# A hand-ordered one-core kernel: the same 633 tasks in another order, 63 of them on another engine

## The chip, the cores and the metric

The kernel runs on one core of one Trainium2 chip. The metric is device time in microseconds (us), median of the runs; lower is better. Five instruction queues matter: PE (TensorE, matmuls; its weight loads are listed as PEld), ACT (ScalarE), DVE (VectorE), POOL (GpSimd) and SP (SyncE, which here only issues DMAs).

## The reference

What is computed, cut to its core: a layer norm of x (2048 rows of 448), a linear recurrence over the rows (a state-space scan) on one branch, a two-layer MLP with a second layer norm on the other, and a gated sum.

```python
def _A_ref(x, ...):                                  # recurrence, L = 2048
    Lam_bar = jnp.exp(dt * Lam)
    B_bar = ((Lam_bar - 1.0) / Lam)[:, None] * Bmat
    Bu = jnp.einsum("bld,pd->blp", x + 0j, B_bar)
    for t in range(L):
        h = Lam_bar[None, :] * h + Bu[:, t, :]
    y = 2.0 * jnp.einsum("blp,dp->bld", hseq, Cmat).real + x * Dskip
def _B_ref(x, w1, b1, w2, b2):                       # MLP, F = 1792
    y = _layernorm(x)
    h = _gelu(jnp.einsum("bsd,df->bsf", y, w1) + b1)
    return jnp.einsum("bsf,fd->bsd", h, w2) + b2
xn = _layernorm(x)
return x + _A_ref(xn, ...) * silu(_B_ref(xn, ...))
```

## The kernel before

The 2048 rows are worked in four groups (g = 0 to 3) of 512 rows: two blocks of 128 partitions with two rows (even and odd, "par") each. The scan runs over pairs of rows, so even and odd rows get different output matrices.

The program is a list of 633 tasks. A task is one or a few instructions of one engine, with the names of what it reads and writes. `link` derives from these names, in the order of creation, which task depends on which. `emit` then issues the tasks in the order of a hand-kept list, `ORDER`; each engine's queue is the subsequence of `ORDER` that belongs to it, and an engine takes its instructions strictly in that order. Tasks added by `either` have two forms for two engines (DVE or ACT, POOL or DVE); the numbers in the list `SECOND` take the second form. Nothing else sets the order: there are no priorities at run time.

Waits are placed by `emit`. A task waits for the semaphore of every task it depends on, except for one shortcut (line 129): a PE task does not wait for an earlier PE task, unless one of them is marked `split`.

```python
for d in sorted(t.deps, key=at.get, reverse=True):
    if t.eng == d.eng == "pe" and not (t.split or d.split):
        continue
    sem, val = done[d]
    if seen.get(sem, 0) < val:
        waits.append((sem, val))
```

The PE tasks that are marked `split` are those of the first MLP product, `mm1_run` (matmul line 801). One pass of it over a group has seven steps j = 0 to 6, and a step fills two PSUM banks (the bank pairs are 0/1, 2/3 and 4/7, used in turn). A step is cut in two phases. The first, called **Fj** below, has six matmuls of 64 weight rows that start the two accumulations; the second, **Sj**, has eight that finish them. The two row halves of the array change banks between Fj and Sj, and both write the same two banks, so Sj depends on Fj and waits for its semaphore. After Sj come two gelus on ACT (line 805), which write `gT`; the next step on the same bank pair depends on them. For group 0 the pass is cut in three: steps 0 to 4 for the first 128-row block (256 columns a matmul; marked a), steps 5 and 6 for both blocks, steps 0 to 4 for the second block (marked b). All other passes have 512 columns. The phases are tasks 113 to 153, 286 to 305, 409 to 428 and 537 to 556.

Other PE tasks: `mm2` (line 828, second MLP product, 14 matmuls, two PSUM banks in turn, drained by DVE line 831), `bu` (line 729, input product of the scan, four tasks a group, all in bank 4, drained into `u_sb` at line 417), `m0` (line 712, a product of CQ and B, once), `ym` (lines 871, 874 and 877, the output product, bank 7 nearly throughout, drained by DVE lines 883, 885 and 888). The scan between `bu` and `ym` is on DVE (lines 744 to 775, with `s_w` scanned at 753). CQ and CZ (line 661) are output matrices with the discretisation worked in, made by DVE and ACT from `Ct0` to `Ct3`, which are DMA transposes issued by SP (line 83), as are `BT` (transposed input matrices), `xnT` and `xmT` (transposed normalised rows; `xmT` is the tile xn2T). SP's plain DMAs (line 84) load x, the weights and B, C, and store the output. `dbc` (a skip vector) is loaded by POOL and halved by task 45 on DVE.

Of the kernel before, what the change touches and what calls it, by code (L numbers as in the profile page):

```python
# [159 lines left out]


ORDER = [int(k) for k in """
# [17 lines left out]
""".split()]  # L180
SECOND = [int(k) for k in """
45 53 54 61 63 66 69 74 76 83 112 130 133 158 160 162 163 165 177 184 185 187 189 190 220 222 224 226 228 230 238 248 249 258 266 268 331 362 364 365
384 400 401 436 447 468 480 482 487 491 499 501 502 504 510 528 529 609 612 627
""".split()]


# [834 lines left out]
```

## Time and profile before

| what | value |
|---|---|
| time, median of 3 runs | 153.23 us (153.21 to 153.32) |
| span of the profiled execution | 151.8 us, 2974 instructions |
| PE busy | 147.1 us (97%), 1127 matmuls |
| DVE busy | 127.6 us (84%) |
| ACT busy | 99.0 us (65%) |
| POOL busy | 42.1 us (28%) |
| granted TensorE clock | full throughout |

The profile is of one execution, whose span from the first to the last instruction is 151.8 us. The 1.4 us to the median lie outside the span; the profile gives no other time of that execution. Times in the views count from the start of the span.

### The profile page before, as it was taken

To read this page: it belongs to the slowest core of one execution; us is meant where nothing else is said; L and a number is where in the kernel's file an instruction comes from. 1 tells how busy PE (TensorE), PEld (TensorE's weight loads), DVE (VectorE), ACT (ScalarE), POOL (GpSimd) and SP (SyncE) were. 2 spreads that over 40 slices of the span, in tenths; PEclk is the share of its full clock that TensorE was granted. 3 is DMA by queue.
4 is the path that set the end of the run, shared out by engine and by line. 5 is a ranking of instruction groups with operands and counts; after the bars stand their busy time and mean duration, and the time that the engine had idled before them with its cause. 6 is when DMAs were issued, how large, how long until landed. Compare 5 with 4: busy or idle time off the path is not lost.

```text
span 151.8 us, 2974 instructions
## 1 busy us (share of the span) xinstructions
PE 147.1 (97%) x1127; PEld 86.6 (57%) x1127; DVE 127.6 (84%) x267; ACT 99.0 (65%) x183; POOL 42.1 (28%) x101
## 2 busy tenths in 40 slices
PE   7899999999999999999999999999999999999992
PEld 7785755454566577545444556764454666555551
DVE  2874999999978979999999996379968726999984
ACT  3888996988789559997898610463579834067400
POOL 5376827153020920010456006200072031000201
PEclk9999999999999999999999999999999999999999
DMA  4999999989997300700003032610331001100022
GB/s 116 262 305 390 266 202 138 219 152 133 165 261 180 65 0 0 138 0 4 0 0 63 4 60 45 154 60 4 60 101 23 0 4 57 64 0 0 4 84 98
DMA packets 31236, 14.73 MB, mean 97 GB/s; under 512 B 24752, under 2 KB 30774, under 8 KB 31222
## 3 DMA queue, kind: packets, MB, share of 16 engines
q1 hardware_dynamic: 30912, 14.26, 41.8%
q0 software_dynamic: 160, 0.23, 1.0%
q8 instruction: 9, 0.15, 0.4%
q10 hardware_dynamic: 150, 0.05, 0.1%
q14 instruction: 5, 0.04, 0.1%
HBM read 6.89 MB, written 1.84 MB: 57 GB/s over the span
## 4 chain that ended last, share of the span: by engine, by line
PE 80%; DVE 9%; DMA 4%; SPq 4%; issue 2%
PE psum L828 23%; PE psum L801 22%; PE psum L729 14%; PE psum L871 13%; DMA x_all<-in_A_x_dram 4%; PE psum L874 4%; SPq L84 4%; PE psum L712 3%; DVE xn_sb L499 2%; DVE lnst L399 1%; DVE s_w L628 1%; PE psum L877 1%; DVE o L831 1%; PE psum L697 1%; DVE tmp L891 1%
## 5 line engine op out<-in xcount | busy, mean ns | idle before, releaser
L801 PE MATMUL psum<-xn2T,w_sb 64*128 64x512 bf16 (+1 forms) x462 | 44.6, 345 | 0.3 <-ACT xn2T L417 0.2
L828 PE MATMUL psum<-w_sb,gT 128*128 128x448 bf16 x224 | 44.5, 353 | 0.2 <-DVE o L831 0.2
L805 ACT ACTIVATE gT<-psum,b1f 128x512 bf16<-128x512 f32 (+1 forms) x66 | 35.9, 625 | 10.4 <-PE psum L801 10.2
L801 PEld LDWEIGHTS psum<-xn2T,w_sb 64*128 64x128 bf16 x462 | 24.1, 109 | 19.8 <-ACT gT L805 2.3
L828 PEld LDWEIGHTS psum<-w_sb,gT 128*128 128x128 bf16 x224 | 21.5, 98 | 20.7 <-DVE o L831 0.6
L417 ACT ACTIVATE u_sb<-psum 128x512 bf16<-128x512 f32 (+2 forms) x22 | 10.5, 478 | 23.0 <-PE psum L729 22.7
L729 PE MATMUL psum<-xnT,BT 128*128 128x256 bf16 x196 | 24.0, 273 | 0.0
L729 PEld LDWEIGHTS psum<-xnT,BT 128*128 128x128 bf16 x196 | 18.9, 98 | 5.4 <-issue 1.1
L891 POOL TENSOR_TENSOR tmp<-t,x_all 128x448 bf16<-128x448 bf16 x5 | 5.2, 1032 | 33.1 <-DVE t L888 30.7
L753 DVE TENSOR_TENSOR_SCAN s_w<-dk,vs 128x774 f32<-128x774 f32 x8 | 14.0, 1760 | 0.1
L500 ACT ACTIVATE xn_sb<-x_all,lnw 128x448 bf16<-128x448 bf16 (+2 forms) x21 | 13.0, 662 | 1.2 <-DVE xn_sb L499 1.1
L417 ACT ACTIVATE vs<-s_w 64x256 bf16<-64x256 f32 (+2 forms) x16 | 10.9, 681 | 2.6 <-DVE s_w L753 1.5
L871 PE MATMUL psum<-CZ,h_sb 128*128 128x448 bf16 x56 | 11.9, 352 | 0.0
L871 PE MATMUL psum<-CQ,h_sb 128*128 128x448 bf16 (+2 forms) x54 | 10.5, 332 | 0.0
L399 DVE BATCH_NORM_STATS2 lnst<-x_all 128x6 f32<-128x448 bf16 x12 | 7.1, 617 | 3.4 <-DMA x_all<-in_A_x_dram 3.4
L831 DVE TENSOR_TENSOR o<-psum,b2bc 128x448 f32<-128x448 f32 x16 | 9.7, 614 | 0.2
L871 PEld LDWEIGHTS psum<-CZ,h_sb 128*128 128x128 bf16 x56 | 5.4, 98 | 4.7 <-DVE lnmv L405 0.4
L871 PEld LDWEIGHTS psum<-CQ,h_sb 128*128 128x128 bf16 x54 | 5.1, 98 | 4.0 <-DVE t L885 0.4
L874 PE MATMUL psum<-M,xnT 128*128 128x448 bf16 x32 | 7.4, 352 | 0.0
L480 POOL TENSOR_TENSOR lnw<-lnw,mhalf 128x8 f32<-128x8 f32 x3 | 7.2, 2404 | 0.3
L883 DVE TENSOR_TENSOR Cr<-psum,xd 128x448 f32<-128x448 f32 x7 | 4.3, 620 | 3.5 <-PE psum L877 3.4
L499 DVE TENSOR_SCALAR xn_sb<-x_all,lnw 128x448 bf16<-128x448 bf16 (+2 forms) x19 | 6.9, 396 | 0.0
(160 smaller groups left out, 189.1 us busy)
## 6 DMA issues: line engine op xcount, KB each, us to landing
out_dram<-tmp SPq DMA_DIRECT2D x7, 224.0 KB, 2.0
x_all<-in_A_x_dram SPq DMA_DIRECT2D x3, 448.0 KB, 4.0
w_sb<-in_B_w_dram SPq DMA_DIRECT2D x3, 448.0 KB, 8.4
w_sb<-in_B_w_dram SPq DMA_DIRECT2D x3, 384.0 KB, 4.8
vs<-in_A_C_re_dram SPq DMA_DIRECT2D x1, 392.0 KB, 11.6
Bn<-in_A_B_im_dram SPq DMA_DIRECT2D x1, 336.0 KB, 10.2
Bn<-in_A_B_re_dram SPq DMA_DIRECT2D x1, 336.0 KB, 10.5
vs<-in_A_C_im_dram SPq DMA_DIRECT2D x1, 336.0 KB, 10.8
```

The source lines that it names most:

```text
L399: dve([lambda e, b=b, par=par, q=q: e.bn_stats(lnst[:, q, :], x_all[:, 2 * g + b, par, :])], [f"x{2 * g + b}"] , [f"st{q}"], 0.62, prio)
L417: kb.either(("act", [lambda e, o=o, i=i: e.activation(o, i, ACT.Copy) for o, i in pairs]), ("dve", [lambda e, o=o, i=i: e.tensor_copy(o, i ...
L499: on = [("dve", [lambda e, o=o, i=i: e.tensor_scalar(o, i, rs, nb, op0=ALU.mult, op1=ALU.add) for o, i in parts], 0.4, 0.12), ("act", [lam ...
L500: ("act", [lambda e, o=o, i=i: e.activation(o, i, ACT.Identity, bias=nb, scale=rs) for o, i in parts], 0.75, 0.2)]
L729: fns = [lambda e, r=r, m=m, d=d: e.matmul(psum[:, 4, r * NK:(r + 1) * NK], BT[:, m, d, :], xnT[:, gx, d, :], start=(d == 0), stop=(d == 6 ...
L753: dve(lambda e, so=so, vi=vi: e.tensor_tensor_scan(so, dk[:].rearrange("p i c -> p (i c)"), vi, 0.0, ALU.mult, ALU.add), ["v", "vl", "dk", ...
L801: return lambda e: e.matmul(view(bk[k]), w1_sb[rows, d, fcol(2 * j + k)], rhs[rows, d, :, :], start=not second and n == 0, stop=second and ...
L805: act([lambda e, k=k: e.activation(gT[:, gb, 2 * j + k, :].rearrange("p (r c) -> p r c", r=2)[:, :, cols], view(bk[k]), ACT.Gelu_apprx_tan ...
L828: fns = [lambda e, fi=fi: e.matmul(psum[:, bk, 0:D], gT[:, gb, fi, q * 128:(q + 1) * 128], w2_sb[:, fi, :], start=(fi == 0), stop=(fi == N ...
L831: dve(lambda e: e.tensor_tensor(o2[:, fb, :], psum[:, bk, 0:D], b2bc[:], ALU.add), [f"ps{bk}", "b2bc"], [f"oo{fb}"], 0.62, prio - 76)
L871: fns = [lambda e, k=k: e.matmul(psum[:, bk, c0:c1], h_sb[:, hb, k, k0:k0 + 128], cm[:, k, c0:c1], start=(k == 0), stop=False) for k in ra ...
L874: fns += [lambda e, d=d: e.matmul(psum[:, bk, c0:c1], xnT[:, gx, d, xs], M0[:, d, c0:c1], start=False, stop=(d == 3)) for d in range(4)]
```

## The change

Only the two lists change. `ORDER` has the same 633 numbers in another order, and `SECOND` loses and gains entries, so that 63 tasks run on the other engine of their two: 20 from DVE to POOL, 14 from POOL to DVE, 16 from ACT to DVE and 13 from DVE to ACT. Most are small (products of four columns, evictions, normalisations). The tasks, their instructions' arithmetic, buffers and dependences are the same.

The core of the diff (three of the 21 lines of `ORDER` on each side, and both `SECOND` lists):

```diff
 ORDER = [int(k) for k in """
-0 13 19 47 9 16 18 20 14 1 94 26 17 95 91 27 92 21 15 24 48 4 96 12 108 93 90 109 97 104 103 25 105 99 22 98 49 50 55 5 51 65 106 2 110 100 111 107 29
...
-382 378 383 364 241 244 375 376 331 379 332 335 239 384 242 385 346 347 188 343 315 336 344 386 349 243 337 246 387 360 312 245 309 348 361 388 355
-365 351 362 160 319 310 352 363 470 247 313 380 356 357 350 390 358 377 409 413 411 410 359 446 403 472 475 412 417 353 389 418 391 414 415 316 473
...
+13 47 14 9 18 15 19 91 92 94 24 95 17 0 1 16 4 93 20 48 21 90 104 105 49 103 96 27 97 108 25 50 55 2 66 22 23 26 106 30 65 3 51 99 109 56 110 98 11
...
+342 187 343 344 375 329 376 381 378 330 382 238 383 331 188 384 348 332 335 379 385 347 244 308 350 315 336 309 471 337 346 473 470 386 474 380 245
+360 472 349 387 313 239 310 446 377 361 362 409 351 476 355 411 388 410 363 242 412 414 413 477 415 449 356 243 357 417 352 418 314 390 353 416 316
...
 SECOND = [int(k) for k in """
-45 53 54 61 63 66 69 74 76 83 112 130 133 158 160 162 163 165 177 184 185 187 189 190 220 222 224 226 228 230 238 248 249 258 266 268 331 362 364 365
-384 400 401 436 447 468 480 482 487 491 499 501 502 504 510 528 529 609 612 627
+23 45 52 53 54 66 73 77 78 80 86 88 110 112 130 133 158 159 160 162 164 189 192 198 220 222 224 226 236 238 246 248 258 266 269 336 378 382 400 401
+432 440 469 479 480 482 499 501 502 505 514 516 525 530 597 601 627
```

What the two orders make of the phases of the first MLP product on PE's queue (other PE tasks that stand between two phases are written as a bar):

| pass | before | after |
|---|---|---|
| group 0 | F1a F2a S1a F0a S2a S0a \| F4a F3a S4a S3a F5 F0b S5 F6 S0b S6 F1b F3b S1b S3b F2b S2b F4b S4b | F0a F1a S0a S1a F2a \| S2a F4a S4a F3a S3a F5 S5 F6 F0b S0b S6 F1b F3b S1b S3b F2b S2b F4b S4b |
| group 1 | F0 F2 S0 F1 S2 S1 F3 F5 S3 S5 F4 F6 S4 \| S6 | F2 S2 F0 S0 F1 S1 F5 F3 S3 S5 F4 S4 F6 \| S6 |
| group 2 | F0 F2 S0 F1 S2 S1 F3 F5 S3 F4 S5 S4 F6 \| S6 | F0 S0 F1 S1 F2 S2 F3 S3 F4 F5 S5 F6 S6 S4 |
| group 3 | F0 F1 S0 S1 F2 F3 S2 F4 S3 S4 F5 F6 S5 S6 | F1 F0 S0 S1 \| F4 F3 F2 S2 S3 S4 F5 S5 F6 S6 |

Other moves that the text speaks of. On PE, the first four phases of group 3 stand ahead of the last `ym` of group 0 (before: behind the last `ym` of group 1); of group 0's `mm2` the one in three parts comes first. On SP, the DMA transposes come in the order xmT, xmT, Ct0, BT3, Ct2, xnT, (a load of B), Ct3, BT0, xnT, BT4, Ct1, BT1 (before: xmT, xmT, xnT, Ct3, xnT, Ct2, Ct0, Ct1, BT0, BT3, BT1, BT4). On DVE, task 45 stands ahead of the layer norm of group 1, and the eviction of the first `mm2` stands between two of its normalisations. On ACT, the absolute value of the angle table (task 177), the copy into `dk` (184) and a B product (192) stand ahead of the second gelu table load of group 1's pass.

28 rows, old and new, of the table ORDER are left out of this document.

## The prediction

> **What bounds the kernel now.** I read the page first, then the shapes by line, the waits, and the timeline of PE.
>
> ```profile
> span 151.8 us, 2974 instructions
> PE 147.1 (97%) x1127; PEld 86.6 (57%) x1127; DVE 127.6 (84%) x267; ACT 99.0 (65%) x183; POOL 42.1 (28%) x101
> PEclk9999999999999999999999999999999999999999
> PE 80%; DVE 9%; DMA 4%; SPq 4%; issue 2%
> ```
>
> PE is busy for 97% of the span at full clock, and the chain that ended last is 80% PE, 121 us of it. No matmul is added or taken away. So an order can win only what PE loses between matmuls, and it loses whatever new gap it puts there. The next question is how large the gaps are now. The waits of PE's weight loads, and the timeline, show the ones that reach PE:
>
> ```profile
> PEld psum L801 <- ACT gT L805: 2.3, 7, 0.5
> PEld psum L801 <- PE psum L801: 0.7, 2, 0.3
> 19.03 8.12 PE L828 MATMUL psum<-w_sb,gT 128*128 128x448 bf16 x42
> 27.33 2.82 PE L828 MATMUL psum<-w_sb,gT 128*128 128x448 bf16 x14 [0.18 <-DVE o L831]
> 30.08 10.11 PE L801 MATMUL psum<-xn2T,w_sb 64*128 64x512 bf16 x90
> 30.08:40.12 10.04, 10.04 (x91) 4.76 (x90) 9.57 (x21) 8.11 (x13) 3.37 (x10) 1.00 0.97 153
> 105.66:116.43 10.77, 10.77 (x99) 5.26 (x98) 8.94 (x14) 7.50 (x12) 3.61 (x4) 1.00 0.29 65
> ```
>
> The last two lines are windows (stretch, its length, then busy time and instructions of PE, PEld, DVE, ACT, POOL, the clock). A pass of the first MLP product takes 0.110 us a matmul in group 3 (10.77 by 98) and 0.112 in group 1 (10.04 by 90): there are some tenths of a us a pass to win, no more. The mm2 at 27.33 stood 0.18 us behind an eviction; since a matmul in a stream starts some 0.16 us before the listed end of the one ahead (the run-out worked out below), that place costs about 0.3. Together I see at most 1 us of gaps that another order could close.
>
> The second line of waits is the one that matters. Twice PE's weight loads waited for PE itself.
>
> **What that wait costs.** PE's tasks do not wait for each other, except the phases of the first product: Sj waits for the semaphore of Fj. Where another phase stands between them the wait is over when it is reached. Where Sj stands directly behind Fj, PE must let Fj run out first. Before, that is so at two places, both at the end of group 0: F2b S2b and F4b S4b. Timeline of PEld, then windows from start to start of neighbouring phases:
>
> ```profile
> 16.86 0.25 PEld L801 LDWEIGHTS psum<-xn2T,w_sb 64*128 64x128 bf16 x6
> 17.45 0.69 PEld L801 LDWEIGHTS psum<-xn2T,w_sb 64*128 64x128 bf16 x14 [0.33 <-PE psum L801]
> 18.47 0.36 PEld L801 LDWEIGHTS psum<-xn2T,w_sb 64*128 64x128 bf16 x8 [0.33 <-PE psum L801]
> 15.34:15.67 0.33, 0.33 (x9) 0.25 (x7) 0.33 (x1) 0.33 (x2) 0.24 (x2) 1.00 1.02 301
> 16.00:16.44 0.44, 0.44 (x12) 0.44 (x10) 0.41 (x2) 0.44 (x2) 0.35 (x2) 1.00 1.07 287
> 16.88:17.45 0.57, 0.51 (x10) 0.24 (x7) 0.57 (x5) 0.57 (x3) 0.49 (x2) 1.00 1.12 244
> 17.45:17.91 0.46, 0.46 (x8) 0.46 (x10) 0.43 (x3) 0.46 (x2) 0.32 (x2) 1.00 1.16 261
> 17.91:18.47 0.56, 0.50 (x10) 0.23 (x7) 0.53 (x2) 0.56 (x2) 0.53 (x2) 1.00 1.29 201
> ```
>
> F1b, with another phase behind it, takes 0.33 us to the next start; F2b and F4b, with their own second phase behind them, 0.57 and 0.56. An eight-matmul phase takes 0.44; S2b, after the stop, 0.46. So one such place costs 0.57 - 0.33 + 0.46 - 0.44 = **0.26 us**, or 0.23 for the second without its restart. I take 0.24.
>
> Those are phases of 256 columns. For 512 columns the trace has no such place.
>
> ```profile
> L801 PE MATMUL psum<-xn2T,w_sb 64*128 64x512 bf16 x322 | 36.5, 377 | 0.0
> L801 PE MATMUL psum<-xn2T,w_sb 64*128 64x256 bf16 x140 | 9.1, 271 | 0.3 <-ACT xn2T L417 0.2
> 30.08:30.74 0.66, 0.66 (x7) 0.32 (x8) 0.61 (x2) 0.25 (x1) 0.00 (x0) 1.00 0.70 139
> 31.39:32.25 0.86, 0.86 (x10) 0.41 (x8) 0.86 (x2) 0.78 (x2) 0.86 (x2) 1.00 0.60 115
> L805 ACT ACTIVATE gT<-psum,b1f 128x512 bf16<-128x512 f32 x46 | 28.3, 687 | 10.0 <-PE psum L801 9.9
> ```
>
> A 256-column matmul lasts 271 ns and a pair of them takes 0.33 by 3 = 110 ns, so 161 ns are run-out that a stream hides. With 512 columns it is 377 ns against 0.66 by 3 = 220 ns, so 157 ns: the same run-out, and I take the same 0.24 us. The bounds: from 0 (if the longer stream covered the wait) to 0.33, the idle time of the weight loads at each of the two places.
>
> The Trainium skill ("TensorE: Matmul & The Clock Gate", section "Single matmul latency") puts an isolated warm matmul at (398 + N)/2.4 ns, 166 ns above its columns. By that figure alone the 19 places counted below would cost an estimated 3.2 us, and the time would be near 156.3; the two places in this trace cost more, since a semaphore and the weight load come after the run-out.
>
> **The change part by part.**
>
> *First product, phases on PE.* Counting Fj directly followed by Sj in the two orders: group 0 has 6 (F4a, F3a, F5, F0b, F2b, F4b; 2 before), group 1 has 5 (F2, F0, F1, F3, F4; 0 before), group 2 has 6 (F0, F1, F2, F3, F5, F6; 0 before), group 3 has 4 (F0, F2, F5, F6; 0 before). That is 21 against 2: 19 more, 16 of them with 512 columns. Nothing on PE can cover them, because the queue is in order; only a wait that PE would have had anyway at the same place can. The gelus do not give that: two of them take 1.27 us (timeline row below, six in 3.58 and four in 2.43 with overlap) against 0.66 + 0.86 = 1.52 of PE a step, and with the stop PE needs 1.76. 19 x 0.24 = **+4.6 us**; bounds 0.7 (the three new 256-column places alone) to 6.3 (19 x 0.33).
>
> ```profile
> 32.94 3.58 ACT L805 ACTIVATE gT<-psum,b1f 128x512 bf16<-128x512 f32 x6
> 37.17 2.43 ACT L805 ACTIVATE gT<-psum,b1f 128x512 bf16<-128x512 f32 x4 [0.64 <-PE psum L801]
> 35.42 2.73 PEld L801 LDWEIGHTS psum<-xn2T,w_sb 64*128 64x128 bf16 x28 [0.46 <-ACT gT L805]
> 31.57 1.28 ACT L618 ACT_TABLE_LOAD   x1
> L631 DVE SCALAR_TENSOR_TENSOR s_w<-s_w 128x1024 f32<-128x1024 f32 x1 | 1.2, 1226 | 0.0
> L646 DVE COPY dk<-cw 128x768 f32<-128x768 f32 x1 | 0.7, 684 | 0.0
> L500 ACT ACTIVATE xn_sb<-x_all,lnw 128x448 bf16<-128x448 bf16 x9 | 6.6, 759 | 0.1
> ```
>
> *mm2 of group 0.* The one in parts goes first and its eviction is early on DVE, so the wait at 27.33 goes: **-0.3**, bounds 0 and -1.0 (all the gaps above).
>
> *ACT ahead of group 1's gelus.* The table load at 31.57 ends 32.85 and the first gelu follows at once; F5 of this pass, whose weight load starts at 35.42, then waited for a gelu. To ACT come the absolute value (1.2 on DVE, about the same here), the dk copy (0.7 on DVE, say 0.85) and a B product (0.67); from it go two normalisations (2 x 0.76) and another B product (0.67). Net some +0.5 us before the first gelu, but PE reaches F5 and F3 about 0.6 later too, by the stops of F2, F0 and F1. I take **+0.2**, from 0 to 0.5.
>
> *The 63 moved tasks.* They balance: DVE loses 33 tasks and gains 30.
>
> ```profile
> L891 DVE TENSOR_TENSOR tmp<-t,x_all 128x448 bf16<-128x448 bf16 x10 | 3.8, 386 | 0.1
> L891 POOL TENSOR_TENSOR tmp<-t,x_all 128x448 bf16<-128x448 bf16 x5 | 5.2, 1032 | 33.1 <-DVE t L888 30.7 <-DMA out_dram<-tmp 2.4
> L417 ACT ACTIVATE vs<-s_w 128x1536 bf16<-128x1536 f32 x4 | 5.9, 1487 | 1.6 <-DVE s_w L753 1.5
> L753 DVE TENSOR_TENSOR_SCAN s_w<-dk,vs 128x774 f32<-128x774 f32 x8 | 14.0, 1760 | 0.1
> ```
>
> A sum that goes to POOL takes 1.03 for 0.39, but POOL is idle for 72% of the span, so its queue rather than its speed counts. The largest newcomer on DVE is the copy of 128x1536 (1.5 on ACT) in group 2's scan; the normalisations and evictions that go the other way pay for it. At 84%, DVE has 24 us free, and a PE that needs 4 us longer gives it four more. I take **0**, from -0.3 to +1.
>
> *SP and the matrices C.*
>
> ```profile
> 29.11 3.96 SPq L83 DMA_TRANSPOSE Cr<-vs x3
> 33.12 6.09 SPq L83 DMA_TRANSPOSE BT<-Bn x4
> Cr<-vs SPq DMA_TRANSPOSE x4, 3.3
> L661 DVE SCALAR_TENSOR_TENSOR CQ<-Cr,cw,tmp 128x448 bf16<-128x448 bf16 x7 | 4.8, 681 | 0.1
> 48.46 1.49 PE L712 MATMUL psum<-CQ,Bn 128*128 128x448 bf16 x7
> ```
>
> A transpose holds SP's queue 1.3 us (3.96 by 3). Before Ct1, the last C that CQ needs, now stand three BT, the second xnT and a load: before, its issue ended at 33.07 and began 1.3 earlier, and with 3.3 us from issue to landing it was there at 35.1. It comes some 4 x 1.3 + 0.6 = 5.8 us later, so CQ starts near 41. Before, CQ had at most 48.46 - 35.1 = 13.4 us to its use by m0, with 27 tasks on DVE's queue from its first step to its last; now there are 22, and PE's use moves back by one mm2 (2.7) and nine stops (2.2) to 53.4. Even with all of the 13.4 it would be 0.9 late. Cost **0**, up to +1.5.
>
> On DVE, task 45 (which waits for a load on POOL's queue) and the eviction of the three-part mm2 now stand ahead of the last normalisations of group 1. That mm2 ends no earlier than 19.03 + 2.7 (a third of 8.12) and four stops of group 0 (1.0), at 22.7, so the xmT transposes behind it are issued near 24. The pass that needs them started at 30.08 and moves to 30.8 (1.0 later, less 0.3); two transposes of 1.3 and a landing of 3.3 make 24 + 1.3 + 3.3 = 28.6: **0**, up to +1.
>
> *The end.* The same last tasks; one add moves off DVE, one store moves behind another. **0**, within 0.2.
>
> **Sum.** 4.6 - 0.3 + 0.2 = +4.5 us on the profiled span: 156.3. The span lies 1.4 us under the median of 153.23, which I keep: **157.7 us**.
>
> **Rivals.**
>
> *Late feeders on top of the stops.* DVE falls behind at C, at the transposes for a pass, or in the scans. For it: the new queues have several places with under 1 us to spare by my sums. Against it: each stop gives DVE, ACT and SP 0.24 us more. It adds 1.5 to 3.5: 159.2 to 161.2. It would show as waits of PEld for DVE or DMA.
>
> *Half of the stops are covered.* The new order puts other ACT tasks between the gelus (a B product and a normalisation in group 1, evictions in group 3). Where gelus then fall behind by 0.24 us a step, PE would wait for the bank anyway. For it: seven waits for gelus now. Against: 0.25 us a step of spare ACT time. Ten stops paid is 2.4: about 155.5.
>
> *The other side: 512-column stops cost nothing.* The longer stream covers the semaphore, so only the three new 256-column stops are paid (+0.7), and the gaps of before go (-1.0): 152.9, faster by 0.3. It decides at the first F2 S2 of group 1: if S2 starts within 0.7 us of F2, it holds, if at 0.9, not. Against it stand the equal run-outs, 157 and 161 ns. A rule that would speak for it is the skill's (same page, section "Step-by-step: what each phase is for") that weight loads are pulled ahead of running matmuls; the trace agrees within a phase, but at both places the load itself sat idle 0.33 us.
>
> **How the numbers follow.** Forecast as summed, 156.6 to 158.9 by its own terms: 0.52. Late feeders: 0.24. Half covered: 0.17. The other side: 0.07, of which half under the 0.2% (0.3 us) that a measurement of this kernel can tell. The range 155.2 to 160.4 leaves out the other side, the lower part of the half-covered case and the worst late feeders. Faster by over 0.2%: 0.04; within: 0.02; slower: 0.94.
>
> **What would show it.** After the change, the line of PEld waiting for PE should read 21 times and 7 to 10 us. A pass of group 2 should take 12.2 us for 98 matmuls where group 3's took 10.77 before. The wait at group 0's mm2 should be gone, the busy times of DVE and ACT within 2 us of before. The prediction is wrong if those waits are there and the span is under 154, or if the extra time sits in waits for DVE or DMA.

## The result, and the profile after

| kernel | median | runs |
|---|---|---|
| before | 153.22 us | 153.21 to 153.32 |
| after | 160.53 us | 160.38 to 160.6 |

The changed kernel is slower: ratio 1.0474, 95% interval 1.0459 to 1.0489, or +7.3 us. The forecast was 157.7, with a range from 155.2 to 160.4. The sign was right, the size was not. In some executions of many kernels here the granted clock falls to about 0.6 for a few us near the start and the time is some 1.5 us longer (one of q1_ct ran at 0.76 and took 199.15 us), so the parts below are read as stretches inside a trace.

The page of the changed kernel: span, busy times, granted clock, and the chain that ended last.

```profile
span 158.8 us, 2974 instructions
PE 151.1 (95%) x1127; PEld 86.0 (54%) x1127; DVE 132.3 (83%) x269; ACT 94.8 (60%) x175; POOL 49.0 (31%) x107
PEclk9999999999999999999999999999999999999999
PE 73%; DVE 15%; issue 3%; DMA 2%; ACT 2%; SPq 2%; POOL 2%; DVEq 0%
```

The span grew by 7.0, PE's busy time only by 4.0; DVE's share of the chain went from 9% to 15%. The waits name the rest (engine, line, waited for; us in total, times, longest):

```profile
PEld psum L801 <- PE psum L801: 9.5, 19, 0.6
PEld psum L871 <- DVE h_sb L775: 1.3, 1, 1.3
PE psum L871 <- DVE h_sb L775: 0.8, 1, 0.8
PEld psum L871 <- DVE Cr L883: 0.8, 1, 0.8
PE psum L871 <- DVE Cr L883: 0.5, 1, 0.5
PE psum L801 <- DMA w_sb<-in_B_w_dram: 0.7, 1, 0.7
```

The first line stood at 0.7 and 2 times before. The other five were not there: two output products (`ym`) that wait for DVE, and a first phase that waits for a load of w1. Windows and timelines of PE show where each lies:

```profile
70.42:82.64 12.22, 11.83 (x100) 4.88 (x99) 12.11 (x26) 9.04 (x18) 5.50 (x11) 1.00 0.01 1
23.61:31.65 8.04, 8.04 (x43) 4.01 (x42) 6.59 (x19) 7.98 (x12) 1.08 (x8) 1.00 0.65 123
7.89 1.72 PE L801 MATMUL psum<-xn2T,w_sb 64*128 64x256 bf16 x28 [0.72 <-DMA w_sb<-in_B_w_dram]
61.54 1.70 PE L729 MATMUL psum<-xnT,BT 128*128 128x256 bf16 x14
100.46 1.50 PE L871 MATMUL psum<-CZ,h_sb 128*128 128x448 bf16 x7 [0.52 <-DVE Cr L883]
148.83 1.31 PE L871 MATMUL psum<-CQ,h_sb 128*128 128x448 bf16 x6 [0.82 <-DVE h_sb L775]
```

The pass of group 2 with its six stops takes 12.22 us, where group 3's took 10.77 before. The last three `mm2` of group 0 run without a gap (8.04 busy of 8.04): the wait of 27.33 is gone.

At three tasks on PE both orders have done the same work ahead, so their starts can be subtracted:

| PE reaches | before | after | lag | added in the stretch |
|---|---|---|---|---|
| the first `bu` of group 0 (323) | 40.12 | 42.76 | +2.63 | nine stops 2.1; start 0.9; the wait at `mm2` -0.35 |
| the first phase of group 2 (409) | 67.57 | 70.42 | +2.86 | small waits for DVE 0.2 |
| a late `ym` of group 3 (616) | 141.92 | 148.83 | +6.91 | ten stops 2.3; `ym` 485 0.7; `ym` 606 and 616 1.1 |

The right column comes from the gaps on PE's timeline: where Sj followed another phase it started 0.16 us ahead of the listed end of the one before, directly behind Fj it starts 0.06 or 0.07 after it, so 0.23 a stop. The experiments test whether these parts are causes, or only waits that something else would have put there anyway.

### The profile page after: what moved, and what is told of

Same layout as the page of the kernel before. It is cut to its first block, busy times and chain, and to the rows that moved or that the text cites. A ratio compares the mean times of both kernels' runs of the same rounds, so it can differ in the third digit from the quotient of the medians.

```text
span 158.8 us, 2974 instructions
## 1 busy us (share of the span) xinstructions
PE 151.1 (95%) x1127; PEld 86.0 (54%) x1127; DVE 132.3 (83%) x269; ACT 94.8 (60%) x175; POOL 49.0 (31%) x107
## 3 DMA queue, kind: packets, MB, share of 16 engines
HBM read 6.89 MB, written 1.84 MB: 55 GB/s over the span
## 4 chain that ended last, share of the span: by engine, by line
PE 73%; DVE 15%; issue 3%; DMA 2%; ACT 2%; SPq 2%; POOL 2%; DVEq 0%
PE psum L801 28%; PE psum L828 18%; PE psum L729 11%; PE psum L871 8%; PE psum L874 3%; PE psum L712 3%; DMA w_sb<-in_B_w_dram 2%; SPq L84 2%; ACT vs L417 2%; POOL xd L847 2%; DVE Cr L883 1%; DVE t L885 1%; DVE pb L772 1%; DVE t L888 1%; DVE pa L771 1%
## 5 line engine op out<-in xcount | busy, mean ns | idle before, releaser
L801 PE MATMUL psum<-xn2T,w_sb 64*128 64x512 bf16 (+1 forms) x462 | 48.1, 347 | 2.5 <-DMA w_sb<-in_B_w_dram 0.7
L805 ACT ACTIVATE gT<-psum,b1f 128x512 bf16<-128x512 f32 (+1 forms) x66 | 36.5, 623 | 15.1 <-PE psum L801 15.0
L801 PEld LDWEIGHTS psum<-xn2T,w_sb 64*128 64x128 bf16 x462 | 23.3, 109 | 26.2 <-PE psum L801 9.5
L417 ACT ACTIVATE u_sb<-psum 128x512 bf16<-128x512 f32 (+2 forms) x19 | 9.3, 492 | 13.0 <-PE psum L729 12.8
L500 ACT ACTIVATE xn_sb<-x_all,lnw 128x448 bf16<-128x448 bf16 (+2 forms) x15 | 9.7, 676 | 11.7 <-POOL xd L847 6.8
L753 DVE TENSOR_TENSOR_SCAN s_w<-dk,vs 128x774 f32<-128x774 f32 x8 | 14.0, 1756 | 0.0
L891 POOL TENSOR_TENSOR tmp<-t,x_all 128x448 bf16<-128x448 bf16 x5 | 8.9, 1778 | 15.8 <-DVE t L888 9.3
L417 ACT ACTIVATE vs<-s_w 64x256 bf16<-64x256 f32 (+2 forms) x15 | 9.3, 627 | 6.6 <-DVE s_w L755 3.4
L847 POOL TENSOR_TENSOR xd<-xn_sb,dbc 128x448 bf16<-128x448 bf16 x6 | 7.7, 1282 | 10.1 <-DVE Cr L883 10.1
L499 DVE TENSOR_SCALAR xn_sb<-x_all,lnw 128x448 bf16<-128x448 bf16 (+2 forms) x25 | 9.3, 406 | 1.2 <-DMA xnT<-xn_sb 1.2
L561 POOL TENSOR_TENSOR cw<-cw 128x4 f32<-128x4 f32 x13 | 3.0, 247 | 13.7 <-DVE cw L561 13.4
```

What stands on the lines that cost most here:

```text
L417: kb.either(("act", [lambda e, o=o, i=i: e.activation(o, i, ACT.Copy) for o, i in pairs]), ("dve", [lambda e, o=o, i=i: e.tensor_copy(o, i ...
L499: on = [("dve", [lambda e, o=o, i=i: e.tensor_scalar(o, i, rs, nb, op0=ALU.mult, op1=ALU.add) for o, i in parts], 0.4, 0.12), ("act", [lam ...
L500: ("act", [lambda e, o=o, i=i: e.activation(o, i, ACT.Identity, bias=nb, scale=rs) for o, i in parts], 0.75, 0.2)]
L753: dve(lambda e, so=so, vi=vi: e.tensor_tensor_scan(so, dk[:].rearrange("p i c -> p (i c)"), vi, 0.0, ALU.mult, ALU.add), ["v", "vl", "dk", ...
L801: return lambda e: e.matmul(view(bk[k]), w1_sb[rows, d, fcol(2 * j + k)], rhs[rows, d, :, :], start=not second and n == 0, stop=second and ...
L805: act([lambda e, k=k: e.activation(gT[:, gb, 2 * j + k, :].rearrange("p (r c) -> p r c", r=2)[:, :, cols], view(bk[k]), ACT.Gelu_apprx_tan ...
```

## The experiments

Each changes nothing but the two lists. Stretch readings are differences of the start of a PE task from its start in the changed kernel (the tasks are numbered as in `ORDER`: F4a is 123, at 10.73; 323 the first `bu` of group 0, 383 the second `bu` of group 1 at 61.54, 409 the first phase of group 2 and 430 the first `ym` behind its pass, 485 and 616 the two late `ym`, 541 a phase of group 3):

| kernel | F4a | 323 | 383 | 409 | 430 | 485 | 541 | 616 |
|---|---|---|---|---|---|---|---|---|
| a1_phases | +1.64 | -0.66 | -0.03 | -0.03 | +2.24 | +2.24 | +2.22 | +3.06 |
| a3_feeders | +1.88 | +1.85 | +1.84 | +1.84 | +1.84 | +1.17 | +1.15 | +1.05 |
| a5_feed | +1.68 | +1.66 | +1.66 | +1.66 | +1.66 | +0.98 | +0.97 | +0.27 |
| q2_ct_ph01 | +0.22 | -0.82 | -0.83 | -0.83 | -0.84 | -0.83 | -0.83 | -0.84 |
| q4_sp_ph01 | +0.33 | -0.39 | -0.38 | -0.39 | -0.39 | -0.39 | -0.39 | -0.39 |
| q5_sp_ph01 | +0.12 | -2.16 | -1.52 | -1.52 | -1.53 | -1.52 | -1.52 | -1.52 |
| l1_start | -0.53 | -0.50 | -0.49 | -0.50 | -0.51 | -0.50 | -0.50 | -0.51 |
| a4_ph23 | +0.38 | +0.35 | +0.35 | +0.35 | -0.83 | -0.48 | -0.48 | -0.48 |
| c3_all | -0.48 | -1.69 | -1.69 | -1.69 | -2.88 | -3.80 | -3.80 | -4.50 |

What a kernel lost or won between two columns is the change from one to the next. The column F4a stands ahead of every edit but those of l1_start and c3_all, so in the other kernels it is the lateness of that execution's start and has to be taken off. a3_feeders shows that such a start is carried on whole: its queues are the changed kernel's as far as 430, and it is 1.84 to 1.88 late all the way.

### What a stop costs, in the kernel before

b1_stops and b2_stops12 put phase orders of the changed kernel into the kernel before:

```diff
 PE, kernel before (gelus on ACT in the same order)
-group 1: F0 F2 S0 F1 S2 S1 F3 F5 S3 S5 F4 F6 S4 | S6
+group 1: F2 S2 F0 S0 F1 S1 F5 F3 S3 S5 F4 S4 F6 | S6
-group 2: F0 F2 S0 F1 S2 S1 F3 F5 S3 F4 S5 S4 F6 | S6
+group 2: F0 S0 F1 S1 F2 S2 F3 S3 F4 F5 S5 F6 S6 | S4
 b1_stops only:
-group 3: F0 F1 S0 S1 F2 F3 S2 F4 S3 S4 F5 F6 S5 S6
+group 3: F1 F0 S0 S1 F4 F3 F2 S2 S3 S4 F5 S5 F6 S6
```

> The kernel before with only the phase orders of the changed kernel in groups 1, 2 and 3: 15 places more where Sj stands directly behind Fj (17 against 2), all of 512 columns; all other queues but the gelus' order as before. Stops theory: 15 x 0.23 = +3.5 us: 153.2 to about 156.7, and a pass of 14 phases 10.8 to about 12.2 us where it has six stops. Covered theory: the gelus or the scan on DVE bound these stretches anyway, so the stops fall into waits that are there: +1 us or less.

> The kernel before with only the phase orders (and gelu orders) of the changed kernel in groups 1 and 2: eleven stops of 512 columns more, nothing else; group 3, where the earlier run had made gelus late, stays as before. Stops theory: 11 x 0.23 = +2.5 us: 153.3 to about 155.8. Rival, the feeders of before have slack enough to give part back later: 155.0 or less.

b1_stops took 159.54 us (ratio 1.0392, 1.0352 to 1.0433): too much. In group 3 its gelus stood in slots made for another order, and PE waited 1.66 us for one (row below), which is a fault of the experiment. Ahead of that its trace has the same two steps as the next run. b2_stops12, without group 3, took 156.0 (ratio 1.0172, 1.0129 to 1.0215), +2.8 for eleven stops; its trace shows +1.05 for the five of group 1 and +1.47 for the six of group 2. First row b1_stops, PE's timeline; second b2_stops12, waits:

```profile
112.93 2.13 PE L801 MATMUL psum<-xn2T,w_sb 64*128 64x512 bf16 x18 [1.66 <-ACT gT L805]
```

```profile
PEld psum L801 <- PE psum L801: 6.6, 13, 0.6
```

Thirteen waits are the eleven new ones and the two of before. So 0.21 to 0.25 us each, all paid where nothing else is late: the stops theory holds, with the size forecast. The Trainium skill's 166 ns ("TensorE: Matmul & The Clock Gate", section "Single matmul latency") stays short of it by a quarter; the trace does not agree with it as the price of such a place.

### The same stops taken out of the changed kernel

```diff
 a1_phases: PE, changed kernel
-group 0: ... F4a S4a F3a S3a F5 S5 F6 F0b S0b S6 ...
+group 0: ... F4a F3a S4a S3a F5 F0b S5 F6 S0b S6 ...
 groups 1 and 2: as before (F4 S5 F6 S4 S6 at the end of group 2)
-group 3: F1 F0 S0 S1 | F4 F3 F2 S2 S3 S4 F5 S5 F6 S6
+group 3: F0 F1 S0 S1 | F2 F3 S2 F4 S3 F5 S4 S5 F6 S6
```

> The changed kernel with only the phases of the first MLP product (and their gelus) taken back to interleaved orders: 18 of the 21 places where Sj stands directly behind Fj are gone (left: F2b S2b, F4b S4b and F6 S6 of group 3). Stops theory: each costs 0.23 us and nothing covers it, so 18 x 0.23 = 4.1 us come back: 160.5 to about 156.4, PEld's wait for PE from 9.5 us to about 1.2. Feeder theory: DVE, ACT and the transposes are the real limit of the changed order and PE only waits elsewhere when the stops go; then at most 2 us come back (158.5 or more) and the waits for DVE grow by the rest.

It took 162.14 us (ratio 1.0535, 1.048 to 1.0589), longer than the changed kernel, though PEld's wait for PE fell from 9.5 to 1.2 us. Its times lie between 160.56 and 163.63, and in the traced one, the longest, the granted clock fell twice, so the total says little. The rows are windows of that trace; the third figure from the end is the clock:

```profile
8.00:12.00 4.00, 3.88 (x38) 3.27 (x40) 2.61 (x11) 2.38 (x5) 1.01 (x4) 0.57 1.02 315
73.00:76.50 3.50, 3.45 (x18) 1.78 (x20) 3.50 (x6) 0.45 (x1) 0.00 (x0) 0.55 0.02 5
```

The stretches say more. The trace was 1.64 us late at F4a and 0.66 ahead at 323, so nine stops gone gave 2.3 us, 0.25 each. At 383 it had kept 1.67 of them. It lost more than that later (2.3 us between 409 and 430, the second fall of the clock included, and 0.8 between 541 and 616), because the orders of before put F2 of groups 2 and 3 early, whose bank pair DVE drains late in the new order (PE's timeline):

```profile
73.05 3.39 PE L801 MATMUL psum<-xn2T,w_sb 64*128 64x512 bf16 x16 [1.84 <-DVE lnmv L405]
117.38 8.05 PE L801 MATMUL psum<-xn2T,w_sb 64*128 64x512 bf16 x70 [1.23 <-DVE Cr L883]
```

Between 323 and 383 it gave up 0.6 of the 2.3: something beside PE came into play there. In the changed kernel SP's queue and DVE show what (SP's timeline, then DVE's):

```profile
25.05 2.71 SPq L83 DMA_TRANSPOSE xn2T<-xn_sb  x2
39.89 1.29 SPq L83 DMA_TRANSPOSE Cr<-vs  x1
42.57 0.58 SPq L84 DMA_DIRECT2D x_all<-in_A_x_dram  x1
```

```profile
39.03 0.69 DVE L661 SCALAR_TENSOR_TENSOR Bn<-Bn,cw,tmp 128x448 bf16<-128x448 bf16 x1 [1.87 <-ACT tmp L658]
42.89 0.81 DVE L659 TENSOR_SCALAR tmp<-Cr,cw 128x448 f32<-128x448 bf16 x2 [1.41 <-DMA Cr<-vs]
49.77 0.62 DVE L831 TENSOR_TENSOR o<-psum,b2bc 128x448 f32<-128x448 f32 x1 [0.54 <-PE psum L828]
```

Ct1 is issued at 39.89 (31.8 before), CQ starts at 42.89 (35.4 before), and from there DVE works until the eviction that 383 waits for with one gap of note, 0.54 us in which it waits for PE. So PE's chain is the later one, and the chain of SP, Ct1 and DVE is about half a us behind it. In a1_phases PE comes earlier, that gap of DVE is gone, and PE waits in its turn (PE's timeline of a1_phases, the rows of 325 and 383):

```profile
44.95 1.69 PE L729 MATMUL psum<-xnT,BT 128*128 128x256 bf16 x14 [0.16 <-DMA BT<-Bn]
61.51 1.70 PE L729 MATMUL psum<-xnT,BT 128*128 128x256 bf16 x14 [0.24 <-DVE u_sb L417]
```

Five kernels shorten one chain or both:

```diff
 q1_ct, q2_ct_ph01: SP and ACT
-SP: ... Ct3 BT0 xnT(167) BT4 Ct1 BT1 x(218) ...
+SP: ... Ct3 Ct1 BT0 xnT(167) BT4 BT1 x(218) ...
-ACT: gelu gelu gelu(292) B-product(198)
+ACT: gelu gelu B-product(198) gelu(292)
 q3_sp, q4_sp_ph01: ACT as above
-SP: xmT xmT Ct0 BT3 Ct2 xnT(166) B(38) Ct3 BT0 xnT(167) BT4 Ct1 BT1 x(218)
+SP: B(38) xmT xmT Ct0 BT3 Ct2 x(218) xnT(166) Ct3 xnT(167) BT0 Ct1 BT4 BT1
 q5_sp_ph01: ACT as in the changed kernel, x(218) behind xnT(166)
 q2, q4, q5: groups 0 and 1 of PE as in a1_phases
```

> The changed kernel with two tasks moved in their queues: on SP the transpose Ct1 (215) directly behind Ct3 instead of behind BT0, xnT and BT4, and on ACT the B product 198, for which DVE waited, ahead of a gelu. CQ on DVE can then start 2 to 3 us earlier than at 42.9. Two-chains theory: in groups 0 and 1 the chain xmT transposes, Ct1, CQ on DVE and the chain of PE with its stops reach the bu at 383 within 0.1 to 0.4 us of each other, so shortening this one alone wins at most that: 160.1 to 160.5. Rival, the stops of group 1 are not on the path at all and DVE's chain is the only one: 1.5 us or more come back, 159.0 or less.

> The changed kernel with SP's queue alone put right: the last B load (38) ahead of the transposes instead of among them, the load of x for groups 2 and 3 (218, which DVE's statistics wait for) 12 places earlier, xnT before BT0 and Ct1 directly behind BT0; and on ACT the B product 198 ahead of a gelu. Two-chains theory: DVE's chain to 383 gets 2 us or more shorter, PE's own chain with its stops is within 0.4 us of it, so at most that is won: 160.1 to 160.5. Rival, DVE's chain is the only one: 159.0 or less.

q1_ct took 160.61 us (ratio 1.0474, 1.0449 to 1.0499), q3_sp 160.61 (1.0469, 1.0425 to 1.0513); the trace of q3_sp is within 0.05 us of the changed kernel's at every task of the table from 323 on. In it CQ starts at 42.09, 0.8 us earlier where 2 or more were expected, and DVE then waits 1.07 us for PE in place of 0.54 (DVE's timeline). The feeder chain alone wins nothing, as the two-chains theory has it.

```profile
49.80 0.62 DVE L831 TENSOR_TENSOR o<-psum,b2bc 128x448 f32<-128x448 f32 x1 [1.07 <-PE psum L828]
```

> The same two moves, and the phases of the first MLP product in groups 0 and 1 interleaved as before (nine of the 21 stops gone). Two-chains theory: now both chains are shorter, and 9 x 0.23 = 2.1 us come back, with 0.1 to 0.4 of the waits that PE had at 330 and 383: 158.1 to 158.4. Stops-alone theory gives 158.4 too, but it also gave the interleaved phases alone 2.1 us at that place, and they brought 0.03. Rival, a third chain (the transposes of B, the normalisations for group 2) is just as long: 159.5 or more.

> The same, with the phases of groups 0 and 1 interleaved (nine stops gone). Two-chains theory with the load 218 as the missing link of the run before: both chains are short now, 2.1 us of stops and 0.2 of waits come back: 158.1 to 158.4, with PE's wait at 383 for DVE gone. Rival, a further feeder holds 383 near 60.7 as before: 0.8 us come back, 159.6.

Both missed: 159.3 and 160.3 us (ratios 1.0393, 1.0348 to 1.0438, and 1.0466, 1.0421 to 1.051). In both traces the moves had made another feeder late, and at 323 only 1.04 and 0.72 us were left with the start taken off. In q2_ct_ph01 Ct1, moved ahead, held back xnT 167; in q4_sp_ph01 the product 198 waited for DVE and held the gelu behind it. Three of the six executions of q2_ct_ph01 took 158.7 to 158.9, about as much under the traced one (159.75) as its wait is long; whether they went without it is not shown. PE's timeline of q2_ct_ph01, then of q4_sp_ph01:

```profile
41.94 1.69 PE L729 MATMUL psum<-xnT,BT 128*128 128x256 bf16 x14 [0.88 <-DMA xnT<-xn_sb]
```

```profile
39.58 0.84 PE L801 MATMUL psum<-xn2T,w_sb 64*128 64x512 bf16 x6 [0.91 <-ACT gT L805]
40.73 1.70 PE L801 MATMUL psum<-xn2T,w_sb 64*128 64x512 bf16 x14 [0.32 <-ACT gT L805]
```

> As the last run with the phases of groups 0 and 1 interleaved, but the B product 198 stays where the changed kernel has it on ACT (there it had held a gelu for 0.9 us) and the load 218 goes behind xnT 166. Two-chains theory: PE reaches the mm2 at 311 two us earlier, CQ on DVE starts 1.4 us earlier, and both arrive at 383 about 1.9 us earlier: 158.5 to 158.8. Rival, yet another feeder takes the place: 159.6 or more, as in the two runs before.

158.93 us (ratio 1.0376, 1.0332 to 1.042), near what was expected. With the start taken off PE reaches 323 2.28 us earlier, which is the nine stops, and 383 and all that follows 1.64 earlier; the rest goes in one wait (PE's timeline):

```profile
40.59 1.70 PE L729 MATMUL psum<-xnT,BT 128*128 128x256 bf16 x14
43.88 1.69 PE L729 MATMUL psum<-xnT,BT 128*128 128x256 bf16 x14 [0.59 <-DMA BT<-Bn]
```

So the stops of groups 0 and 1 are paid in the changed kernel. Taken out, they give back 1.64 us at 383 with SP's queue moved and 1.67 without (a1_phases, one trace with its late start taken off), out of 2.3. The other 0.65 is the feeders': mostly DVE's in a1_phases, a late BT's in q5_sp_ph01.

### Groups 2 and 3, the start, and the late output products

```diff
 a4_ph23: PE
-group 2: F0 S0 F1 S1 F2 S2 F3 S3 F4 F5 S5 F6 S6 S4
+group 2: F0 F1 S0 S1 F2 F3 S2 F4 S3 F5 S5 F6 S4 S6
-group 3: F1 F0 S0 S1 ...
+group 3: F0 F1 S0 S1 ...
```

> The changed kernel with the phases of group 2 in the order F0 F1 S0 S1 F2 F3 S2 F4 S3 F5 S5 F6 S4 S6 (one stop instead of six; F2 as late as in the changed kernel, since bank 7 comes free late there) and the first four of group 3 as F0 F1 S0 S1 (one stop gone); nothing else moved. Stops theory: behind 61.5 us PE is the path again, so 6 x 0.23 = 1.4 us come back: about 159.1. Rival, the output products and the scan on DVE hold the end whatever PE does: under 0.5 us, 160.0 or more.

160.11 us (ratio 1.0433, 1.0412 to 1.0453). The pass of group 2 gave 1.18 us for five stops, 0.24 each (+0.35 at 409, -0.83 at 430), and the stop of group 3 another 0.26 just ahead of 485. Then `ym` 485 took 0.6 of it back: its wait for DVE went from 0.52 to 1.13 us (row below). The stops theory holds in the passes; the rival holds at 485.

```profile
99.98 1.50 PE L871 MATMUL psum<-CZ,h_sb 128*128 128x448 bf16 x7 [1.13 <-DVE Cr L883]
```

```diff
 l1_start (a2_loads: the same, but x's two loads exchanged as well, the copy on ACT, gelus not moved)
-SP: w1_0 w1r_1 w1r_0 w1_1 w1r_2 w1_2 ...
+SP: w1_1 w1r_1 w1_0 w1r_0 w1_2 w1r_2 ...
-PE: F0a F1a S0a S1a F2a ... S2a
+PE: F1a F2a S1a F0a S2a S0a ...
 ACT: gelus of S1a, S0a, S2a in this order; copy 23 back on DVE behind the b1 columns
```

> The changed kernel with only its start taken back: SP's loads of w1 in the order of before (slice 1, then 0, 2, 3), the first six phases F1a F2a S1a F0a S2a S0a, and the copy of slice 0's small part later on ACT. First-loads theory: in the changed kernel PE stood 0.72 us for slice 1 and was 0.9 us late at F4a; that goes, -0.9 us: about 159.6. Rival: PE is held by when slice 2 lands, whatever the order ahead of it, or later waits take the gain up: 160.2 to 160.5.

> The changed kernel with only its start as before: w1's loads in the order of slice 1, 0, 2, 3, the first six phases F1a F2a S1a F0a S2a S0a and their gelus in that order, the copy of slice 0's small part on DVE behind the b1 columns; the loads of x as in the changed kernel. First-loads theory: F4a starts 0.9 us earlier, and since mm2's first eviction, the transposes and DVE's chain all hang on PE in group 0, all of it is carried to the end: about 159.6. Rival, DVE's chain hangs on the loads of B and C and not on PE: 160.3 to 160.6.

a2_loads took 161.14 us (ratio 1.0486, 1.0445 to 1.0526), a miss: its first normalised rows came 0.45 us later on DVE (4.87 against 4.42) and its first phase 0.75 later. It differs from l1_start in x's loads, the copy and the gelus, and which of them did it was not separated. l1_start took 160.03 (ratio 1.0433, 1.039 to 1.0477). The first phase of PE no longer waits for w1, and the 0.5 us it wins at F4a stays 0.5 to the end. PE's timeline of l1_start:

```profile
6.95 2.77 PE L801 MATMUL psum<-xn2T,w_sb 64*128 64x256 bf16 x42
10.20 0.52 PE L801 MATMUL psum<-xn2T,w_sb 64*128 64x256 bf16 x6
```

Of the 0.9 us that the changed kernel lags there, 0.5 is shown to be the loads' order; 0.4 stays unexplained (the landings of the first loads differ by some tenths from run to run).

```diff
 a3_feeders, a5_feed: ACT and DVE
-ACT: xn(501) sb(397) sb3(398) sf3(399)
+ACT: sb(397) sb3(398) sf3(399) xn(501)
-DVE: ym-evict(596) g(467) vl(530) mm2-evict(461) ...
+DVE: mm2-evict(461) vl(530) ym-evict(596) g(467) ...
 a3_feeders: g(463) ahead of pa(579)
 a5_feed: sf3(586) ahead of mm2-evict(560) and ym-evict(604)
```

> The changed kernel with four tasks moved in their queues: on ACT a normalisation of group 3 (501, which waits for a POOL sum) behind the scan's state copies (397 to 399); on DVE two tasks that are ready (461, 530) ahead of 596, at which DVE stood 2.45 us, and 463 ahead of 579. Queue theory: the waits of ym 485 (0.68 us) and ym 616 (0.98 us) go: -1.6 us, about 158.9. Rival: DVE is simply too full in these stretches, the order within the queue matters little and another task is late next: -0.5 us or less, 160.0 or more.

> The changed kernel with the waits before the output products of DVE alone undone: normalisation 501 behind the scan's copies on ACT; on DVE 461 and 530 ahead of 596, and 586 ahead of the evictions 560 and 604, so that ACT's copy 588 does not come last. Queue theory: 0.7 us at ym 485 and 0.8 at ym 616 come back: about 159.0. Rival, DVE is full there and the order matters little: only the 0.7 at 485 that a run before showed, 159.8.

a3_feeders took 159.79 us (ratio 1.0425, 1.037 to 1.048): `ym` 485 won 0.67, 616 only 0.1, because 463 then waited 1.47 us for ACT. a5_feed had a median of 160.79 (ratio 1.0436, 1.038 to 1.049); its executions took 159.26 to 162.4, and the traced one was 1.68 late at F4a. In its trace the late products give 0.68 at 485 and 0.70 more by 616, so 1.4 in all; a new wait at 606 takes 0.25 of what 616 wins (PE's timeline):

```profile
145.12 1.31 PE L871 MATMUL psum<-CQ,h_sb 128*128 128x448 bf16 x6 [0.25 <-DVE t L888]
149.10 1.30 PE L871 MATMUL psum<-CQ,h_sb 128*128 128x448 bf16 x6
```

### The engines of the 63 tasks

s1_engines is the changed order with the `SECOND` of before, o1_engines the order of before with the `SECOND` of the change.

> The order of the changed kernel with the engines of before for all 63 tasks. As predicted for the engines: no difference beyond 0.3 us, 160.2 to 160.8. Late-feeder theory: the sums of x and D on POOL (up to 2.4 us each) and the copies that went from ACT to DVE make the two late output products; with the old engines 0.7 to 1.5 us come back: 159.0 to 159.8. Rival, the order was made for the new engines and gets longer with the old ones: 161 or more.

> The kernel before, its order untouched, with the engines of the changed kernel for the 63 tasks: the mirror of the run that gave the changed order the old engines (+7.3 us). As predicted for the engines: -0.3 to +1, 153.0 to 154.3. Fit theory: an order is fitted to its engines, and a mismatch costs several us whichever way: 156 or more, as waits of PE for DVE or ACT.

s1_engines took 167.84 us (ratio 1.0955, 1.0906 to 1.1003), o1_engines 173.12 (1.1277, 1.1232 to 1.1321). Both are far from the prediction's zero for the engines, and going back to the old ones won nothing; what held is that an order is fitted to its engines. What the 63 moves cost in the order made for them neither run can say, since each puts the engines into an order made for others. In o1_engines two C products (230 and 228) that had been DVE's stand on ACT's queue ahead of the gelus of group 1; they wait for DVE, the gelus wait behind them, PE waits for a gelu. ACT's timeline, then PE's wait:

```profile
41.71 0.67 ACT L658 ACTIVATE tmp<-Cr,cw 128x448 f32<-128x448 bf16 x1 [5.20 <-DVE CQ L661]
44.01 0.67 ACT L658 ACTIVATE tmp<-Cr,cw 128x448 f32<-128x448 bf16 x1 [1.63 <-DVE CQ L661]
44.58 2.98 ACT L805 ACTIVATE gT<-psum,b1f 128x512 bf16<-128x512 f32 x5
```

```profile
PE psum L801 <- ACT gT L805: 8.4, 1, 8.4
```

Two products of 0.67 us, in a queue not made for them, stand in front of 8.4 us of waiting on PE. That is read from the trace: no run moved these two alone.

### Everything together, and the one gain of the change

c1_all has q1_ct's moves, groups 0 and 1 interleaved, a4_ph23, the start of l1_start but for the gelus and copy 23, and a5_feed's moves. c3_all takes q5_sp_ph01's SP queue, groups 0 and 1, and all of l1_start instead.

> All of it at once in the changed kernel: Ct1 and the B product earlier, 15 of the 21 stops gone, w1's loads and the first six phases in the order of before (the two loads of x as in the changed kernel), the normalisation 501 behind the scan's copies on ACT, and on DVE 461 and 530 ahead of 596 and 586 ahead of two evictions. Sum theory: 15 x 0.23 = 3.4, the first loads 0.9, ym 485 0.7, ym 616 0.8, PE's small waits 0.4: -6.2, about 154.3, so that what is left of the change is worth some +1 us. Rival, another feeder is late next in two or more of these places: 156 or more.

> All repairs together in the changed kernel: SP's order and interleaved groups 0 and 1 as in the first kernel of this call, the start as before, the six stops of group 2 and the first of group 3 down to one, and the feeders of the output products. Sum of what the runs showed: 1.9 (groups 0 and 1) + 0.5 (start) + 1.4 (groups 2 and 3) + 1.5 (feeders) = 5.3: 155.2, some 2 us over before. Rival, the repairs overlap as in the first run of all at once (156.8), with another feeder late: 156.5 or more.

156.83 us (ratio 1.0224, 1.0201 to 1.0247) and 155.63 (1.015, 1.0109 to 1.0191). So 4.9 of the 7.3 us are undone by naming them. What is left, from the trace of c3_all: four stops more than before (0.9), 0.4 at the start, and two waits for gelus in group 1 (0.37 and 0.31 us idle, with the 0.16 of overlap lost at each about 1.0): PE now comes earlier, and ACT, with its tables and table load ahead, starts that pass's gelus no earlier than 33.9. No combination came below the kernel before.

```diff
 d1_evict: DVE, kernel before
-B-products(192, 193) ... mm2-evict(274) ...
+mm2-evict(274) B-products(192, 193) ...
```

> The kernel before with one task moved: on DVE the eviction 274 of the mm2 in parts ahead of the B product 192, so that the mm2 at 27.33 finds its bank free. That is the one gap of the kernel before that the changed order closes. As predicted: -0.3 us, 152.9. Rival, the feeders of the bu at 383 or the gelus take it up: 153.2.

153.39 against 153.34 us in the same session (ratio 1.0025, 0.9993 to 1.0057). The gap at 27.33 is gone in the trace and PE gains 0.35 us there, but the profiled execution had started 0.25 us later than the one of before; a gain of this size cannot be told from the spread of the start.

## Why the prediction was wrong

**The stops: right.** 0.23 us each against 0.24, 19 waits and 9.5 us of PEld against 21 and 7 to 10, a pass of group 2 of 12.22 against 12.2. The term of 4.6 us measures 4.4 by the gaps on PE: nine stops 2.1 at 323 (2.3 in a1_phases and q5_sp_ph01), six at 0.24, four at 0.23 in group 3, of which a4_ph23 undid one. That nothing covers them is right but for groups 0 and 1, where 1.65 of 2.3 came back.

**The 63 moved tasks at 0: the step that failed.** Apart from the last tasks this was the only term for how DVE, ACT and POOL feed the output products, and it argued from idle shares: POOL is idle for 72% of the span and DVE has 24 us free. It called POOL's queue the thing that counts, but did not follow one here. What counted was who stands behind whom, which the new `ORDER` sets as well as the engines. For `ym` 485 the trace gives the whole way (POOL's, DVE's and ACT's timeline of the changed kernel):

```profile
89.61 2.42 POOL L847 TENSOR_TENSOR xd<-xn_sb,dbc 128x448 bf16<-128x448 bf16 x1 [1.55 <-DVE Cr L883]
89.44 1.76 DVE L753 TENSOR_TENSOR_SCAN s_w<-dk,vs 128x774 f32<-128x774 f32 x1
91.12 1.39 DVE L885 SCALAR_TENSOR_TENSOR t<-Cr,g_sb 128x448 bf16<-128x448 f32 x1
92.06 0.76 ACT L500 ACTIVATE xn_sb<-x_all,lnw 128x448 bf16<-128x448 bf16 x1 [6.79 <-POOL xd L847]
92.73 2.63 ACT L417 ACTIVATE vs<-s_w 128x1536 bf16<-128x1536 f32 x4
```

A product with `dbc` (468) that went from DVE to POOL took 2.42 us, not 1.03. ACT stood behind it, 6.79 us idle in all, with a normalisation (501) that nobody needed yet; the scan's copies (397 to 399), ready at 91.2, stood behind that; DVE waited for them, and the product waited for DVE. The normalisation was ACT's before too: the new `ORDER` took it from behind these copies to ahead of them. At 616 the same kind of thing: DVE stood 2.45 us at 127.84 before an eviction (596) whose product was not done, with two ready tasks behind it. One of them, 461, had stood ahead of 596 in the kernel before, on the same engine; the other, 530, had been POOL's. Moving such tasks back in their queues, with all 63 engines left as they are, returned 1.4 us (a5_feed). The page showed each engine's idle share, and I read spare time off it; the time was there, but not at the head of the queue.

**The start: a term that was missing.** The prediction did not look at the first loads. Slice 1 of w1 went from fourth to seventh place on SP's queue and PE waited 0.72 us for it: 0.9 us of lag, 0.5 of it shown by l1_start, the rest open.

**SP and the matrices C at 0: right as a sum, wrong as a picture.** CQ was to start near 41 and started at 42.89. It costs next to nothing (q3_sp; the waits for DVE up to 409 are 0.2 in all), but it made a second chain half a us behind PE's, so that taking out the stops alone leaves 0.6 of their 2.3 us behind at 383 (a1_phases). I had set these late tasks against PE's own delay, which was the right account; but it leaves little slack to anyone who wants to repair one side.

**The small terms.** The wait at 27.33 went (right, -0.35 in the trace). ACT ahead of group 1's gelus was put at +0.2 and cost nothing; c3_all, where the stops and the late start no longer hold PE back, has two gelu waits there. The end cost nothing beyond 616.

**The rivals.** Late feeders on top of the stops, at 159.2 to 161.2, is what came, with 0.24 given to it against 0.52 for the plain sum; of the places that it named the scans were right, since both late products stand behind a scan's copies or its `h_sb`; C and the transposes cost 0.2, and the first loads it did not name. The half-covered case did not come: all 19 waits are there. The other side fell at the first F2 S2 of group 1: S2 starts 0.91 us after F2 (31.65 to 32.56 on PE's timeline), the value that the prediction had named against it. The late products and the start are 2.3 us that stood in the sum as 0.

## What to carry to other kernels

In a kernel of in-order queues, first count the tasks that stand directly behind the task they wait for on the same engine: each cost 0.21 to 0.26 us here. Then, for every task that changes engine, read what stands behind it in its new queue and who waits for that: an idle share of 70% says nothing about the head of the queue, and two products of 0.67 us stood in front of 8.4 us of waiting. Undoing one cause of several gives only part of it back where a second chain arrives a few tenths later. So subtract the starts of common tasks from trace to trace, stretch by stretch, and take off first what the execution was late before the edit: a1_phases, 1.6 us longer in total, had won 2.3 us where its edits began.

## What the hardware showed beside

The sums and products of 128 x 448 on POOL, 1.03 us in the kernel before, took 2.42 us three times in the changed one, each time with a scan (L753) begun on DVE 0.16 or 0.17 us earlier (89.44 and 89.61 above); behind that scan DVE's next instruction took 1.39 where its like takes 0.62. When POOL began first, DVE was held: a CQ product of 0.68 took 1.40 beside a POOL product begun at 51.69 (DVE's timeline of the changed kernel):

```profile
51.79 1.40 DVE L661 SCALAR_TENSOR_TENSOR CQ<-Cr,cw,tmp 128x448 bf16<-128x448 bf16 x1
```

The Trainium skill ("SBUF — State Buffer", section "Who interferes with whom") has VectorE and GpSimd share one pair of ports, held by whoever issues first for the whole instruction, if the VectorE instruction reads two inputs from SBUF. The rows agree with it: a scan of 1.76 and a sum of 1.03 would end 2.62 us after the sum's start if the one waited for the whole of the other, and 2.42 was measured. So a sum moved to POOL also costs DVE, up to 0.8 us a time.
